# Three heads of the last projection group by twelve GpSimd transfers, dealt over the 16 DMA engines

## The chip, the cores and the metric

One core of one Trainium2 chip. The metric is the device time of one execution in microseconds, the median over runs. Each run also lists the span of that execution, from its first to its last recorded instruction.

## The reference, cut to what matters

A decode step for 4 sequences: `xn = layernorm(x)`; a query projection; attention of 32 query heads over the last 1024 positions of an 8-head cache; an output projection `wo` (4096 x 512); beside it a gated MLP; `out = x + s * g`. Nearly everything read is weights and cache, 28.8 MB, each byte once. The part that changes is the end of the `wo` product:

```python
s = o.reshape(B, Sq, Hq * Dh) @ wo     # wo: 4096 x 512; a group of 4 heads is 512 rows
g = silu(mlp(xn)); return x + s * g
```

## The kernel before

The program builds one list of operations for each engine; SyncE (SP) issues nearly all loads, 28 of 33. The rows of `wo` for group 7, the last of eight, are loaded in two ways: heads 0 to 2 (384 rows) in two even transfers that come last of all, head 3 (128 rows) early, in two small transfers that the trace shows on only 5 and 3 of the 16 DMA engines.

```python
    R3 = (7 * 512 + 384) * D
    d_wox = [pg.dma("sp", "wox%d" % p0, lambda e, p0=p0, n=n, b0=b0: e.dma_start(
        wox_sb[p0:p0 + 4 * n, :, :].rearrange("p j o -> p (j o)"),
        bass.AP(A_wo.tensor, R3 + b0 * D, [[4 * D, n], [4 * n * D, 4], [1, 4 * D]])),
        t_q) for p0, n, b0 in ((0, 5, 0), (32, 3, 80))]
    # ... groups 0 to 6 of wo, then:
    w3_r = A_wo[7 * 512:7 * 512 + 384, :].rearrange("(p i) o -> p i o", i=3)
    d_w3 = [(i0, i1, pg.dma("sp", "w3%d" % i0, lambda e, i0=i0, i1=i1: e.dma_start(
        wo_sb[:, 7, i0:i1, :], w3_r[:, i0:i1, :]))) for i0, i1 in ((0, 2), (2, 3))]
```

The rows land scattered over partitions, so small matmuls with 0/1 matrices (`sel3`, `selx`, built by GpSimd) bring the attention output into the same order. GpSimd otherwise builds masks and issues one transfer:

```python
    c_fold = add("gp", lambda e: e.memset(fold[:, :], 0.0))
    for k in range(4):
        c_fold = add("gp", lambda e, k=k: e.affine_select(...), c_fold)
    # ... x16: 12 rows by ACT, 4 rows by GpSimd
```

The softmax here doesn't subtract the row's maximum and nothing guards it: scores larger than these inputs give would overflow.

## Time and profile before

| | before |
|---|---|
| median time | 76.76 us (three runs, 76.57 to 76.77) |
| span in the profile | 75.05 us |
| time minus span | 1.72 us |
| HBM read | 28.85 MB, 384 GB/s over the span |
| GpSimd: instructions on the page / records in the trace | 24 / 39 |

The page counts only the instructions that keep an engine busy; the trace's records include waits, register moves and drains. The prediction shows the lines on which the reading rests. Three things are to be seen: the DMA engines hardly idle until 70 us (8 or 9 tenths busy in every slice from the second to the thirty-seventh, a share of 1.02 at 70.00 to 70.25); seven of the 16 end by 70.2 us and eight at 71.2 or later; the last matmuls wait for the last transfer.

### The profile page before, as it was taken

The numbers are of one execution on the slowest core, as the hardware profiler recorded it, in microseconds if no ns is written. First come the engines' busy times: TensorE is split into PE (matmuls) and PEld (weight loads), VectorE is DVE, ScalarE is ACT, GpSimd is POOL, SyncE is SP. The second block draws the span as 40 slices with busy tenths as digits, with TensorE's granted clock in tenths as the row PEclk, the third lists the DMA queues.
The fourth block names the chain that finished last, engine by engine and source line by source line (L and its number), as shares of the span: only waits on it lengthen the run. The fifth ranks groups of instructions, "written<-read, shape, count | busy, mean of one in ns | idle before, by whom it ended". The sixth has DMA issues, their size and how long they took to land.

```text
span 75.0 us, 2351 instructions
## 1 busy us (share of the span) xinstructions
PE 51.5 (69%) x1045; PEld 41.3 (55%) x1045; DVE 40.6 (54%) x85; ACT 12.5 (17%) x21; POOL 8.5 (11%) x24
## 2 busy tenths in 40 slices
PE   0000650959999999299999969870869976784670
PEld 0000300259899998299999739640359555573640
DVE  0778200036879997099999606999601664610020
ACT  0611000090003303300330326550030000000000
POOL 6999630000000000000000000000000000000000
PEclk9999999999999999999999999855555555555555
DMA  0999999999999989999999999999999999999700
GB/s 20 262 419 422 430 445 402 420 428 437 419 475 391 466 380 415 432 424 428 424 432 432 415 419 473 401 420 422 424 424 419 419 413 426 421 421 417 277 13 2
DMA packets 4281, 28.94 MB, mean 386 GB/s; under 512 B 526, under 2 KB 658, under 8 KB 1715
## 3 DMA queue, kind: packets, MB, share of 16 engines
q1 hardware_dynamic: 4200, 28.84, 92.3%
q8 instruction: 5, 0.08, 0.4%
q10 hardware_dynamic: 42, 0.01, 0.1%
q0 software_dynamic: 32, 0.00, 0.0%
q14 instruction: 2, 0.01, 0.0%
HBM read 28.85 MB, written 0.00 MB: 384 GB/s over the span
## 4 chain that ended last, share of the span: by engine, by line
PE 22%; DMA 22%; SPq 6%; DVE 3%; ACT 2%; issue 1%
DMA wo_sb<-in_A_wo_dram 22%; PE psK L398 10%; SPq L676 6%; PE psS L418 4%; PE psO L437 2%; PE psK L529 1%; PE psS L444 1%; PE psS L414 1%; DVE kt_buf L539 1%; DVE den_sb L454 1%; PE psM L692 1%; ACT P_buf L426 1%; ACT kt_buf L538 1%; PE psS L714 1%; PE psK L533 0%
## 5 line engine op out<-in xcount | busy, mean ns | idle before, releaser
L404 DVE COPY kt_buf<-psK 128x1024 bf16<-128x1024 bf16 x32 | 20.8, 689 | 3.9 <-PE psK L398 3.9
L398 PE MATMUL psK<-ident,kv_buf 128*128 128x128 bf16 x256 | 20.2, 230 | 1.4 <-PEq L101 1.4
L398 PEld LDWEIGHTS psK<-ident,kv_buf 128*128 128x128 bf16 x256 | 16.2, 104 | 1.5 <-issue 1.4
L418 PE MATMUL psS<-qR,kt_buf 128*128 128x16 bf16 x256 | 10.6, 170 | 0.0
L418 PEld LDWEIGHTS psS<-qR,kt_buf 128*128 128x128 bf16 x256 | 9.7, 97 | 1.3 <-issue 0.3
L437 PEld LDWEIGHTS psO<-P_buf,kv_buf 128*128 128x128 bf16 x256 | 7.7, 102 | 3.6 <-issue 1.9
L437 PE MATMUL psO<-P_buf,kv_buf 128*128 128x16 bf16 x256 | 8.0, 173 | 1.6 <-PEq L101 1.3
L426 ACT ACTIVATE P_buf<-psS 128x512 bf16<-128x512 f32 x8 | 4.8, 597 | 21.9 <-PE psS L418 21.9
L454 DVE TENSOR_REDUCE den_sb<-psS 128x16 f32<-128x512 f32 x8 | 5.5, 682 | 1.3 <-PE psS L444 1.2
L692 PE MATMUL psM<-OW,wo_sb 128*128 128x4 bf16 x124 | 4.2, 167 | 2.3 <-DMA wo_sb<-in_A_wo_dram 2.3
L486 PE MATMUL psO<-wq_sb,xT 128*32 128x512 bf16 x32 | 3.8, 627 | 2.9 <-DMA wq_sb<-in_A_wq_dram 2.7
L470 PE MATMUL psS<-ident,xn_bf 4*128 4x4 bf16 x4 | 0.3, 173 | 7.9 <-DVE y_bf L377 7.9
L692 PEld LDWEIGHTS psM<-OW,wo_sb 128*128 128x128 bf16 x124 | 3.8, 105 | 2.8 <-DMA wo_sb<-in_A_wo_dram 2.5
L470 PEld LDWEIGHTS psS<-ident,xn_bf 4*128 4x128 bf16 x4 | 0.2, 114 | 7.9 <-DVE y_bf L377 7.9
L444 PE MATMUL psS<-P_buf,ones_bf 128*128 128x512 bf16 x8 | 4.3, 534 | 0.0
L492 DVE CAST q_sb<-psO 128x512 bf16<-128x512 f32 x1 | 0.7, 691 | 6.5 <-PE psO L486 6.5
L563 PE MATMUL psK<-w_sb,hT 128*4 128x512 bf16 (+1 forms) x14 | 1.9, 623 | 2.6 <-DMA w_sb<-in_B_w_dram 2.6
L486 PEld LDWEIGHTS psO<-wq_sb,xT 128*32 128x32 bf16 x32 | 0.9, 128 | 5.0 <-DMA wq_sb<-in_A_wq_dram 3.6
L414 PE MATMUL psS<-negm,ind 128*128 128x512 bf16 x8 | 3.3, 411 | 0.0
L710 DVE TENSOR_TENSOR sg_sb<-psM,g_sb 128x16 f32<-128x16 f32 x1 | 0.2, 185 | 5.6 <-PE psM L692 5.6
L448 ACT ACTIVATE P_buf<-P_buf 128x512 bf16<-128x512 bf16 x4 | 2.4, 621 | 1.6 <-PE psS L444 1.6
L563 PEld LDWEIGHTS psK<-w_sb,hT 128*4 128x4 bf16 (+1 forms) x14 | 0.6, 107 | 3.4 <-DVE rden L457 3.1
(82 smaller groups left out, 41.9 us busy)
## 6 DMA issues: line engine op xcount, KB each, us to landing
kv_buf<-in_A_k_cache_dram SPq DMA_DIRECT2D x8, 1024.0 KB, 12.4
kv_buf<-in_A_v_cache_dram SPq DMA_DIRECT2D x8, 1024.0 KB, 12.0
wq_sb<-in_A_wq_dram SPq DMA_DIRECT2D x2, 2048.0 KB, 9.6
w_sb<-in_B_w_dram SPq DMA_DIRECT2D x2, 1792.0 KB, 22.1
wo_sb<-in_A_wo_dram SPq DMA_DIRECT2D x3, 1024.0 KB, 16.3
wo_sb<-in_A_wo_dram SPq DMA_DIRECT2D x1, 512.0 KB, 19.0
wo_sb<-in_A_wo_dram SPq DMA_DIRECT2D x1, 256.0 KB, 16.6
wo_sb<-in_A_wo_dram SPq DMA_DIRECT2D x1, 128.0 KB, 14.7
```

Of the source, the lines that this page charges most:

```text
L398: last = pe.transpose(psK[n % NB][:, j * 128:(j + 1) * 128], kv_buf[:, lg, u * UT + j, :], ident[:, :])
L404: cp[r, n] = bank[n % NB] = add("dve", lambda e: e.tensor_copy(kt_buf[:, n % NKT, :], psK[n % NB][:, 0:1024]), t, kt_user[n % NKT], cls="cp")
L414: pe.matmul(psS[lg % 2][:, 0:512], ind[:, :], negm[:, :], start=True, stop=False, skip_group_check=True)
L418: last = pe.matmul(psS[lg % 2][:, c * 16:(c + 1) * 16], kt_buf[:, n % NKT, j * 128:(j + 1) * 128], qR[:, lg * 16:(lg + 1) * 16], start=Fal ...
L426: ex[g] = add("act", lambda e: e.activation(P_buf[:, g, :], psS[lg % 2][:, 0:512], AF.Exp, scale=SCALE), sc[r, n], cls="ex")
L437: last = pe.matmul(pso[:, 0:16], kv_buf[:, NG + lg, c, :], P_buf[:, lg, c * 16:(c + 1) * 16], start=(c == 0), stop=(c == NC - 1))
L444: den[g] = add("pe", lambda pe: pe.matmul(psS[g % 2][:, 0:512], ones_bf[:, :], P_buf[:, lg, :], start=True, stop=True))
L454: v = add("dve", lambda e: e.tensor_reduce(den_sb[:, cs], bass.AP(psS[g % 2], 0, [[512, 128], [1, 16], [16, NC]]), AX.X, ALU.add), den[g])
L486: last = pe.matmul(psO[m // 4][32 * s:32 * s + 32, 0:512], xT[:, c, :], wq_sb[:, c, m * 512:(m + 1) * 512], start=(c == 0), stop=(c == 3), ...
L563: last = pe.matmul(psK[1][32 * i:32 * i + m, 0:1024].bitcast(F32), hT[:, k, 0:m], w2_sb[:, k, :], start=(k < 4), stop=(k >= FC - 4), tile_ ...
L676: d_wo.append((g0, g1, i0, i1, pg.dma("sp", "wo%d" % n, lambda e: e.dma_start(wo_sb[:, g0:g1, i0:i1, :], wo_r[:, g0:g1, i0:i1, :]))))
L692: last = pe.matmul(psM[:, PS_W + c * 4:PS_W + (c + 1) * 4], w[:, c * 128:(c + 1) * 128], o, start=(st and c == 0), stop=sp, skip_group_che ...
```

## The change

The last even transfer shrinks to head 0, and heads 1 to 3 come early in twelve GpSimd transfers whose slowest dimensions (3, 2, 3, 2, 4, 2, twice) add to 32. The intent, as I read it, is that they go round the 16 engines twice. The rows a partition, 5, 3 or 1, then set how much an engine gets, 40, 24 or 8 KB. The engines that an instruction fetch delayed in the kernel before are apparently meant to get little. For room, the ring of transposed K tiles goes from 10 to 8, and the four rows of `x16` that GpSimd loaded go to ACT.

```diff
-    NKT = 10
+    NKT = 8
-        x16[i:n, :], x_r[i:n, :])) for q, i, n in (("act", 0, 12), ("gp", 12, 16))]
+        x16[i:n, :], x_r[i:n, :])) for i, n in ((0, 12), (12, 16))]          # both by ACT
-    d_wox = [... "sp" ... for p0, n, b0 in ((0, 5, 0), (32, 3, 80))]
+    for p0, n, r in ((0, 3, 5), (12, 2, 3), (20, 3, 1), (64, 2, 1), (72, 4, 5), (88, 2, 1)):
+        XS.append((p0, n, r, b0))
+        b0 += 4 * n * r
+    XS = [(p0 + 32 * h, n, r, b + 192 * h) for h in range(2) for p0, n, r, b in XS]
+    d_wox = [pg.dma("gp", "wox%d" % p0, lambda e, ...: e.dma_start(
+        wox_sb[p0:p0 + 4 * n, 0:r, :].rearrange("p j o -> p (j o)"),
+        bass.AP(A_wo.tensor, R1 + b * D, [[r * D, n], [n * r * D, 4], [1, r * D]])), t_q)
+        for p0, n, r, b in XS]
+    c_sx = add("gp", lambda e: e.memset(selx[:, :, :, :], 0.0))
+    # ... and 14 affine_selects on GpSimd that fill selx (sel3 and its select go)
-    d_w3 = [...]                                # 384 rows, two transfers
+    d_w1st = pg.dma("sp", "w1st", lambda e: e.dma_start(
+        wo_sb[:, 7, 0, :], A_wo[7 * 512:7 * 512 + 128, :]))
```

(The row-selecting matmuls and the projection's small matmuls follow the new layout.)

More of the change, by code (lines that the diff above doesn't have):

```diff
@@ L214, in bass_recurrent_scan__sliding_block_cached__mixer_channel_mlp__decode_kernel @@
     w2_sb = sb([128, FC, D], BF16)
-    wox_sb = wq_sb[0:44, 0, 0:4 * D].rearrange("p (j o) -> p j o", j=4)
+    wox_sb = wq_sb[:, 0, 0:5 * D].rearrange("p (j o) -> p j o", j=5)
     kt_buf = sb([128, NKT, UT * 128], BF16)
@@ L255, in bass_recurrent_scan__sliding_block_cached__mixer_channel_mlp__decode_kernel @@
     OW = sb([128, 4, 28], BF16)
-    sel3 = sb([128, 3, 3, 128], BF16)
-    selx = sb([128, 4, 44], BF16)
-    OW3 = sb([128, 12], BF16)
-    OWx = sb([44, 16], BF16)
+    selx = sb([128, 3, 5, 128], BF16)
+    OWx = sb([128, 20], BF16)
     hT = sb([128, FC, 32], BF16)
@@ L343, in bass_recurrent_scan__sliding_block_cached__mixer_channel_mlp__decode_kernel @@
         base=0, channel_multiplier=-1), c_o32)
-    ones_w = bass.AP(ones_bf, 0, [[128, 128], [0, 9], [1, 128]])
-    c_sel3 = add("gp", lambda e: e.affine_select(
-        sel3[:, :, :, :], ones_w, [[-128, 3], [1, 3], [3, 128]], ALU.is_equal, 0.0,
-        base=0, channel_multiplier=-1), c_1)
-    c_sx = add("gp", lambda e: e.memset(selx[:, :, :], 0.0))
-    for p0, n, b0 in ((0, 5, 0), (32, 3, 80)):
-        c_sx = add("gp", lambda e, p0=p0, n=n, b0=b0: e.affine_select(
-            selx[:, :, p0:p0 + 4 * n], ones_bf[:, 0:16 * n], [[1, 4], [4, n], [4 * n, 4]],
-            ALU.is_equal, 0.0, base=b0, channel_multiplier=-1), c_1, c_sx)
     c_fold = add("gp", lambda e: e.memset(fold[:, :], 0.0))
@@ L365, in bass_recurrent_scan__sliding_block_cached__mixer_channel_mlp__decode_kernel @@
     a = add("act", lambda e: e.activation(sq1[:, :], vt1[:, :], AF.Sqrt), v)
-    d_x16 = [pg.dma(q, "x16%d" % i, lambda e, i=i, n=n: e.dma_start(
-        x16[i:n, :], x_r[i:n, :])) for q, i, n in (("act", 0, 12), ("gp", 12, 16))]
+    d_x16 = [pg.dma("act", "x16%d" % i, lambda e, i=i, n=n: e.dma_start(
+        x16[i:n, :], x_r[i:n, :])) for i, n in ((0, 12), (12, 16))]
     v = add("dve", lambda e: e.reciprocal(rstd1[:, :], sq1[:, :]), a)
@@ L610, in bass_recurrent_scan__sliding_block_cached__mixer_channel_mlp__decode_kernel @@
     mlp1()
-    R3 = (7 * 512 + 384) * D
-    d_wox = [pg.dma("sp", "wox%d" % p0, lambda e, p0=p0, n=n, b0=b0: e.dma_start(
-        wox_sb[p0:p0 + 4 * n, :, :].rearrange("p j o -> p (j o)"),
-        bass.AP(A_wo.tensor, R3 + b0 * D, [[4 * D, n], [4 * n * D, 4], [1, 4 * D]])),
-        t_q) for p0, n, b0 in ((0, 5, 0), (32, 3, 80))]
+    R1 = (7 * 512 + 128) * D
+    XS, b0 = [], 0
+    for p0, n, r in ((0, 3, 5), (12, 2, 3), (20, 3, 1), (64, 2, 1), (72, 4, 5), (88, 2, 1)):
+        XS.append((p0, n, r, b0))
+        b0 += 4 * n * r
+    XS = [(p0 + 32 * h, n, r, b + 192 * h) for h in range(2) for p0, n, r, b in XS]
+    d_wox = [pg.dma("gp", "wox%d" % p0, lambda e, p0=p0, n=n, r=r, b=b: e.dma_start(
+        wox_sb[p0:p0 + 4 * n, 0:r, :].rearrange("p j o -> p (j o)"),
+        bass.AP(A_wo.tensor, R1 + b * D, [[r * D, n], [n * r * D, 4], [1, r * D]])), t_q)
+        for p0, n, r, b in XS]
+    c_sx = add("gp", lambda e: e.memset(selx[:, :, :, :], 0.0))
+    for p0, n, r, b in XS:
+        for j in range(3):
+            if b < 128 * j + 128 and b + 4 * n * r > 128 * j:
+                c_sx = add("gp", lambda e, p0=p0, n=n, r=r, b=b, j=j: e.affine_select(
+                    selx[:, j, 0:r, p0:p0 + 4 * n], ones_bf[:, 0:4 * n * r],
+                    [[1, r], [r, n], [n * r, 4]], ALU.is_equal, 0.0,
+                    base=b - 128 * j, channel_multiplier=-1), c_1, c_sx)
     psx = psS[0]
@@ L638, in fn @@
             o = 7 * 16
-            for a in range(4):
-                last = pe.matmul(psx[0:44, 160 + a * 4:164 + a * 4], selx[:, a, :],
-                                 OTb[:, o + 12:o + 16], start=True, stop=True)
-            for i in range(3):
+            for a in range(5):
                 for j in range(3):
-                    last = pe.matmul(psx[:, 128 + i * 4:132 + i * 4], sel3[:, j, i, :],
-                                     OTb[:, o + j * 4:o + j * 4 + 4],
+                    last = pe.matmul(psx[:, 160 + a * 4:164 + a * 4], selx[:, j, a, :],
+                                     OTb[:, o + 4 + 4 * j:o + 8 + 4 * j],
                                      start=(j == 0), stop=(j == 2))
             return last
-        t = add("pe", fn, ep[HKV - 1], c_sel3, c_sx)
-        return [add("dve", lambda e: e.tensor_copy(OWx[:, :], psx[0:44, 160:176]), t),
-                add("dve", lambda e: e.tensor_copy(OW3[:, :], psx[:, 128:140]), t)]
+        t = add("pe", fn, ep[HKV - 1], c_sx)
+        return add("dve", lambda e: e.tensor_copy(OWx[:, :], psx[:, 160:180]), t)
     for g in range(HKV):
@@ L680, in bass_recurrent_scan__sliding_block_cached__mixer_channel_mlp__decode_kernel @@
         load_wo(n, g0, g1, 0, 4)
-    w3_r = A_wo[7 * 512:7 * 512 + 384, :].rearrange("(p i) o -> p i o", i=3)
-    d_w3 = [(i0, i1, pg.dma("sp", "w3%d" % i0, lambda e, i0=i0, i1=i1: e.dma_start(
-        wo_sb[:, 7, i0:i1, :], w3_r[:, i0:i1, :]))) for i0, i1 in ((0, 2), (2, 3))]
+    d_w1st = pg.dma("sp", "w1st", lambda e: e.dma_start(
+        wo_sb[:, 7, 0, :], A_wo[7 * 512:7 * 512 + 128, :]))
     def wo(tiles, *deps):
@@ L701, in bass_recurrent_scan__sliding_block_cached__mixer_channel_mlp__decode_kernel @@
         if g0 == 0:
-            row_x, row_3 = rows_last()
-            wo([(wox_sb[:, a, :], OWx[:, a * 4:(a + 1) * 4], False, False) for a in range(4)],
+            row_x = rows_last()
+            wo([(wox_sb[:, a, :], OWx[:, a * 4:(a + 1) * 4], False, False) for a in range(5)],
                row_x, *d_wox)
-    for i0, i1, d in d_w3:
-        t_w = wo([(wo_sb[:, 7, i, :], OW3[:, i * 4:(i + 1) * 4], False, i == 2)
-                  for i in range(i0, i1)], d, row_3)
+    t_w = wo([(wo_sb[:, 7, 0, :], OTb[:, 7 * 16:7 * 16 + 4], False, True)], d_w1st,
+             ep[HKV - 1])
     v = add("dve", lambda e: e.tensor_tensor(
```

## The prediction

Read beside it: "instruction fetch" is my word for a packet of the queues that the profile labels instruction; *k* is the number of engines that a transfer uses, and the engine numbers are my names, since no record names an engine. For the kernel before, the trace's completions bear the slowest dimension out as the count for SyncE's and ScalarE's transfers (3, 4, 5 and 12 completions for dimensions of 3, 4, 5 and 12, besides one at the issue). GpSimd's one transfer shows 16 completions for four rows, so they don't tell its k; that GpSimd's k follows the slowest dimension too, and that its transfers take the engines one after the other, was an assumption. The forecast's sum: -0.18 + 0.09 = -0.09 us, called -0.1. Rival 1 is that GpSimd's transfers put one partition on an engine, as the one in the trace did. And the "table load" at 41.6 us is an 8 KB packet of the instruction queue: ScalarE's two table loads are at 1.96 and 15.69 us.

> **What bounds the kernel now.** I read the page's slices first, then the queue lines, then the end of the chain that ended last, then the DMA share of the last two microseconds in quarter-microsecond windows.
>
> ```profile
> DVE  0778200036879997099999606999601664610020
> POOL 6999630000000000000000000000000000000000
> PEclk9999999999999999999999999855555555555555
> DMA  0999999999999989999999999999999999999700
> ...
> q1 hardware_dynamic: 4200, 28.84, 92.3%
> q8 instruction: 5, 0.08, 0.4%
> ```
>
> The DMA row is full from the second slice to the thirty-seventh. The 16 DMA engines never starve, so the span is the start, plus the bytes, plus what happens when the bytes run out. The queue lines show who else uses those engines: five instruction fetches of 16 KB. The POOL row shows that GpSimd has nothing to do after 11 us, so work put there later is free unless someone waits for it.
>
> The chain of waits ends in the output projection's weights:
>
> ```profile
> 55.08 16.56 DMA wo_sb<-in_A_wo_dram
> 71.64 0.05 issue
> 71.68 0.61 PE psM L692 x12
> 72.29 0.03 issue
> 72.32 0.20 DVE sg_sb L710
> ```
>
> So the last two transfers decide the end, and only 12 matmuls and a short tail come after. The windows view (columns: window, its length, busy us of PE, PEld, DVE, ACT, POOL, clock, DMA share, GB/s) shows how the transfers end:
>
> ```profile
> 70.00:70.25 0.25, 0.25 (x16) 0.25 (x14) 0.00 (x0) 0.00 (x0) 0.00 (x0) 0.50 1.02 369
> 70.25:70.50 0.25, 0.25 (x16) 0.25 (x13) 0.00 (x0) 0.00 (x0) 0.00 (x0) 0.50 0.56 221
> 70.50:70.75 0.25, 0.25 (x12) 0.22 (x9) 0.00 (x0) 0.00 (x0) 0.00 (x0) 0.50 0.51 197
> 70.75:71.00 0.25, 0.06 (x3) 0.00 (x0) 0.00 (x0) 0.00 (x0) 0.00 (x0) 0.50 0.53 201
> 71.00:71.25 0.25, 0.21 (x7) 0.21 (x8) 0.00 (x0) 0.00 (x0) 0.00 (x0) 0.50 0.47 168
> 71.25:71.50 0.25, 0.25 (x15) 0.25 (x11) 0.00 (x0) 0.00 (x0) 0.00 (x0) 0.50 0.32 111
> 71.50:71.75 0.25, 0.20 (x7) 0.12 (x5) 0.00 (x0) 0.00 (x0) 0.00 (x0) 0.50 0.04 12
> ```
>
> All engines are busy until 70.2, then the share drops to half at once and stays there until 71.5. Half of the engines finish 1.4 us before the others. This raggedness is all that the change can win: the idle engine time in these rows spread over 16 engines.
>
> The trace's packet records allow more. Within an engine a packet starts 4 ns before the one before it ends, so the packets can be strung into 16 sequences, and all 16 fit what the program gives an engine. I call the four kinds by their load and their end of data. (a) Three engines with 8 packets of 4 KB of the extra wo rows end at 71.36, 71.22 and 71.21. (b) Two with 4 such packets end at 70.54 and 71.41. (c) Seven others end at 70.06 to 70.20. (d) Four others end at 71.48, 71.50, 71.59 and 71.63. Each engine of (d) was hit once by an instruction fetch (at 22.9, 29.2, 48.0, 56.7 us; the packet takes 0.88 to 0.95 us and slows its neighbour, so the engine stays some 1.4 us behind to the end). The later one of (b) was hit by a table load at 41.6. The fifth fetch, at 70.07, fell on an engine of (c) that had just finished. The mean end is 70.80, the last 71.63: perfect balance would give 0.83 us, the upper limit of any such change.
>
> [...] The trace agrees for the hardware queue: the extra rows (slowest dimension 5, then 3) show 5 and 3 engine completions. For GpSimd it shows one transfer only, four 256 B rows on four engines, the same four that hold the input row[...]
>
> **The change, part by part.** Bytes stay the same: the last group's 512 rows of 1 KB. Before, 384 rows come in two even transfers (24 KB an engine) and 128 rows go to engines 0 to 4 (32, 32, 32, 16, 16 KB). After, one even transfer of 128 rows (8 KB an engine) comes last, and the twelve GpSimd transfers add, if their k is 3, 2, 3, 2, 4, 2 twice around: 40 KB on engines 0 to 2 and 10 to 13, 24 KB on 3 and 4, 8 KB on 5 to 9, 14 and 15. So engines 10 to 13 carry 24 KB more and the twelve others 8 KB less. Of (d), two engines are among 12 to 15 and two among 4 to 11 (by whether they took part in a transfer of 12 rows); so the seven light engines are surely meant to be those that fetches hit, and I assume they are.
>
> Per packet the sequences step 42 ns (1 KB), 80 (2 KB), 155 (4 KB), 305 (8 KB), so about 5 ns + 37.6 ns per KB; I estimate 117 for 3 KB and 193 for 5 KB. The cost by engine:
> - Removed everywhere: 8 packets of 2 KB, 0.65 us. Removed on (a): 8 of 4 KB, 1.25; on (b): 4, 0.63.
> - Added: 8 packets of 5 KB, 1.54 us; of 3 KB, 0.94; of 1 KB, 0.34.
> - Added everywhere: GpSimd's small packets. The one such transfer of before put 28 packets of 4 B beside its 4 data packets, two for each engine without data, each 6 ns. Twelve transfers: 12 + 10 packets, 0.13 us.
>
> Sums: (d) -0.65 + 0.34 + 0.13 = -0.18, ends at 71.30 to 71.45. (a) 71.36 - 1.25 - 0.65 + 1.54 + 0.13 = 71.13. (b) 71.41 - 0.63 - 0.65 + 0.94 + 0.13 = 71.20. Engines 10 to 13, from 70.20: -0.65 + 1.54 + 0.13, 71.2. The last end moves from 71.63 to 71.45: the slow four still end last, and they lose only 8 KB.
>
> Then the tail. Before, data ending at 71.63 landed at 71.97, and the last 4 matmuls ended at 72.28, 0.31 later. After, the last transfer is 0.345 us behind group 6 (that is what its 8 packets of 1 KB took before), but group 6's 16 matmuls take 0.43 us from first start to last start. So the last 4 no longer wait for their own data: 0.04 + 0.43 + 4 x 0.027 + 0.17 = 0.75 us after group 6 lands, that is 0.40 after the last landing. The tail grows by 0.09. Net: -0.18 + 0.09, some -0.1 us.
>
> Off the path: 13 row-selecting matmuls become 15, the projection's 28 small matmuls 24, one DVE copy goes; these lie near 66 us, with a wait of 1.5 us for weights after them. At the start GpSimd loses the 1.4 us and 2 x 0.45 us selections. Its new work starts when the q matmuls end (15 us): 12 transfers x 0.7 us (the one of before took 0.68), a memset (about 1.9 us by 528 ns for 512 columns) and 15 selections x 0.4 us, done near 32 us and needed at 65. The smaller K ring (8 of 10) does not bind: a slot is reused 8 units on, scores lag 3.
>
> **The rivals.**
> 1. [...]one partition an engine, always from engine 0. Then engines 0 to 7 carry 32 KB, 8 to 11 22 KB, 12 to 15 10 KB. A slow engine among 5 to 7 gets -0.65 + 1.26 + 0.1 = +0.7, the time some 77.5. For it: the one transfer seen fell on the first four engines. Against: rows and destinations are laid out as if k followed the dimension[...].
> 2. The fetches fall on other engines or at other times, since the instruction streams change. One hit on an engine carrying 40 KB ends near 71.2 + 1.4 = 72.6: 77.7. Against: the code up to the last stage hardly changes, so the first four should stay.
> 3. The small packets cost nothing beside big ones and the tail does not grow: -0.31 us, 76.45.
> 4. GpSimd's work slows the K copies. Before, DVE waits 1.4 us at 30 us for a late K transfer, and the V loads are issued at 46 us for engines that reach them near 50; a delay of 2 us is absorbed. Time unchanged.
>
> **Range and chances.** The main line gives 76.76 - 0.1 = 76.66, say 76.65; I give it some 65%, rival 3 15%, rivals 1 and 2 together 15%. The runs of before spread by 0.2. Range 76.3 to 77.1. Faster by 2% needs 1.5 us, more than perfect balance: 0.01. Slower by 2% needs a fetch on a loaded engine and more: 0.03. Within 2%: 0.96.
>
> **What would show it.** Right: the DMA share falls later but more steeply (above 0.8 until 70.8, gone by 71.5), four engines still end last, the last data 0.1 to 0.3 us earlier, the last 20 matmuls one run. Wrong: engines ending in another pattern (rival 1), a fetch followed by an engine that ends after 72 (rival 2), the DMA row showing a gap in the middle (rival 4).

## The result, and the profile after

| | before | after |
|---|---|---|
| median time | 76.77 us (four runs, 76.57 to 76.78) | 77.03 us (four runs, 76.98 to 77.07) |
| span in the profile | 75.05 us | 75.04 us |
| time minus span, that execution | 1.72 | 2.03 |
| GpSimd: page / records | 24 / 39 | 46 / 61 |

The ratio is 1.004, with a 95% interval of 1.0023 to 1.0058. Ratios here are the mean time of one kernel's fast runs over that of the other's fast runs of the same rounds, so not quite the ratio of the medians. The change is 0.26 us slower, little but clear of noise, and the profiled span did not grow at all.

First the inside of the span. The end of the transfers, in the same windows as before (window, length, busy us of PE, PEld, DVE, ACT, POOL, clock, DMA share, GB/s):

```profile
70.00:70.25 0.25, 0.00 (x0) 0.00 (x0) 0.00 (x0) 0.00 (x0) 0.00 (x0) 0.50 0.81 332
70.25:70.50 0.25, 0.16 (x6) 0.16 (x6) 0.00 (x0) 0.00 (x0) 0.00 (x0) 0.50 0.76 311
70.50:70.75 0.25, 0.25 (x15) 0.25 (x13) 0.00 (x0) 0.00 (x0) 0.00 (x0) 0.50 0.78 311
70.75:71.00 0.25, 0.25 (x15) 0.25 (x13) 0.00 (x0) 0.00 (x0) 0.00 (x0) 0.50 0.67 242
71.00:71.25 0.25, 0.25 (x14) 0.25 (x11) 0.00 (x0) 0.00 (x0) 0.00 (x0) 0.50 0.69 221
71.25:71.50 0.25, 0.11 (x5) 0.02 (x1) 0.00 (x0) 0.00 (x0) 0.00 (x0) 0.50 0.12 41
```

Twelve engines, about three quarters, now work until 71, where it was half before; four end near 70. That is the balance that was intended. The end of the chain of waits (start, us, what):

```profile
52.35 19.17 DMA wo_sb<-in_A_wo_dram
71.52 0.05 issue
71.57 0.70 PE psM L689 x20
72.27 0.02 issue
72.30 0.20 DVE sg_sb L706
```

The last matmuls are now one run of 20 behind group 6's landing, and VectorE's product starts at 72.30 where it started at 72.32. The product won 0.02 us, the whole span 0.01. GpSimd's row on the page and its queue:

```profile
POOL 6994000089999872000000000000000000000000
...
q0 software_dynamic: 608, 0.40, 1.7%
q8 instruction: 5, 0.08, 0.4%
q14 instruction: 1, 0.01, 0.0%
```

Its new work (15 to 29 us) is over long before anyone needs it, and the twelve transfers put 0.40 MB on its queue, 384 rows of 1 KB and small packets. Nothing in these views tells why the execution took 0.3 us longer: that time lies before the first or behind the last instruction record. All four runs show it, with a time minus span of 1.98 to 2.16.

The packed trace holds one thing more that no view prints: semaphore events, and these go on behind the last instruction record. The semaphores from 7 to 255 are each written once there (247 of the 249 have a record in either kernel's trace), and then nine events on semaphore 2 close the execution. In the kernel before, the last four of these nine come 1.81, 1.84, 1.88 and 1.92 us behind the last record; in the changed kernel 1.81, 2.11, 2.14 and 2.19. So 0.26 of the 0.3 us is one late step in that closing exchange, at the very end and not at the start.

### The profile page after: what moved, and what is told of

Read it like the earlier page. It is cut to its first block, busy times and chain, and to the rows that moved or that the text cites. A ratio compares the mean times of both kernels' runs of the same rounds, so it can differ in the third digit from the quotient of the medians.

```text
span 75.0 us, 2371 instructions
## 1 busy us (share of the span) xinstructions
PE 50.3 (67%) x1043; PEld 40.5 (54%) x1043; DVE 40.6 (54%) x84; ACT 12.5 (17%) x21; POOL 17.8 (24%) x46
## 4 chain that ended last, share of the span: by engine, by line
DMA 26%; PE 19%; DVE 3%; SPq 2%; ACT 2%; issue 1%
DMA wo_sb<-in_A_wo_dram 26%; PE psK L383 8%; PE psS L403 4%; PE psO L422 3%; SPq L674 2%; PE psK L514 1%; PE psM L689 1%; PE psS L399 1%; DVE kt_buf L524 1%; DVE den_sb L439 1%; ACT P_buf L411 1%; ACT kt_buf L523 1%; PE psS L429 1%; PE psS L710 1%; PE psK L518 0%
## 5 line engine op out<-in xcount | busy, mean ns | idle before, releaser
L607 POOL DMA_DIRECT2D wq_sb<-in_A_wo_dram x12 | 6.7, 604 | 8.5 <-PE psO L471 8.5
L689 PE MATMUL psM<-OW,wo_sb 128*128 128x4 bf16 x112 | 3.6, 167 | 2.3 <-DMA wo_sb<-in_A_wo_dram 2.3
L689 PEld LDWEIGHTS psM<-OW,wo_sb 128*128 128x128 bf16 x112 | 3.3, 104 | 2.6 <-DMA wo_sb<-in_A_wo_dram 2.5
L615 POOL TENSOR_SCALAR_AFFINE_SELECT selx<-ones_bf 128x8 bf16<-128x8 bf16 (+4 forms) x14 | 4.0, 282 | 1.0
```

The source lines that it names most:

```text
L607: d_wox = [pg.dma("gp", "wox%d" % p0, lambda e, p0=p0, n=n, r=r, b=b: e.dma_start(wox_sb[p0:p0 + 4 * n, 0:r, :].rearrange("p j o -> p (j o)"),
L615: c_sx = add("gp", lambda e, p0=p0, n=n, r=r, b=b, j=j: e.affine_select(selx[:, j, 0:r, p0:p0 + 4 * n], ones_bf[:, 0:4 * n * r], [[1, r], ...
L689: last = pe.matmul(psM[:, PS_W + c * 4:PS_W + (c + 1) * 4], w[:, c * 128:(c + 1) * 128], o, start=(st and c == 0), stop=sp, skip_group_che ...
```

## The experiments

Each job ran the kernel before on the same chip. Over its 42 fast executions in four jobs the mean time minus span was 1.74 to 1.77. The runs list spans to 0.1 us, so means of the difference are good to a few hundredths. The last column is what the theories are about; rows are in the order of the runs.

| kernel | GpSimd records | mean time | mean span | time minus span |
|---|---|---|---|---|
| before (9 runs, first job) | 39 | 76.66 | 74.90 | 1.76 |
| after (4) | 61 | 77.03 | 74.97 | 2.05 |
| one semaphore (5) | 61 | 76.98 | 74.88 | 2.10 |
| spare semaphores (5) | 39 | 76.68 | 74.92 | 1.76 |
| tiny GpSimd transfers (5) | 51 | 76.84 | 75.04 | 1.80 |
| before (11, second job) | 39 | 76.77 | 75.03 | 1.74 |
| 20 memsets first (4) | 59 | 77.03 | 75.00 | 2.03 |
| 2 memsets last (6) | 41 | 76.73 | 75.00 | 1.72 |
| selections first (6) | 61 | 77.01 | 74.97 | 2.04 |
| no GpSimd transfer (4) | 49 | 82.01 | 80.27 | 1.73 |
| before (11, third job) | 39 | 76.78 | 75.05 | 1.74 |
| after, shortened (5) | 47 | 77.36 | 75.60 | 1.76 |
| before, shortened (6) | 26 | 76.76 | 75.02 | 1.74 |
| 16 memsets (2) | 55 | 76.78 | 75.05 | 1.73 |
| 60 memsets (2) | 99 | 76.82 | 75.10 | 1.72 |
| before (11, fourth job) | 39 | 76.77 | 75.00 | 1.77 |
| after, 38 memsets (6) | 99 | 77.41 | 75.67 | 1.74 |

The theories at the start: the 0.3 us outside the span goes with the number of semaphores (S), with the number of GpSimd transfers (G), or with the length of GpSimd's instruction stream (I).

**One semaphore for the twelve** (on the changed kernel).

```diff
-        ... [[r * D, n], [n * r * D, 4], [1, r * D]])), t_q)
+        ... [[r * D, n], [n * r * D, 4], [1, r * D]])), t_q, sem=s_wox)   # waited at 16 * 12
```

> The changed kernel with one semaphore for the twelve GpSimd transfers (11 semaphores fewer than changed, 2 fewer than before); transfers, balance and span unchanged. Theory S (the added time lies outside the profiled span and goes with the number of semaphores: 9 more cost 0.28 us, 0.03 each): span 75.0, time minus span back from 2.03 to about 1.7, time near 76.7. Theory G (it goes with the number of GpSimd transfers) or I (with GpSimd's longer instruction stream): time stays at 77.0.

Measured: 76.96 us median, 2.10 outside. Eleven semaphores fewer bring nothing back: S falls.

**Nine spare semaphores** (on the kernel before).

```diff
+        for i in range(9):
+            nc.alloc_semaphore("spare%d" % i)
```

> The kernel before with nine semaphores allocated and never used, so that the last one has the number it has after the change. Theory S in the form that the highest number or the allocated count matters: 76.77 + 0.28 = 77.05, span unchanged at 75.0. Theory S in the form that only semaphores that are used matter, theories G and I: 76.77.

Measured: 76.70, ratio to before 1.0003, 1.76 outside. S falls from the other side too.

**Twelve tiny GpSimd transfers** (on the kernel before).

```diff
+    d_tiny = [pg.dma("gp", "tiny%d" % i, lambda e, i=i: e.dma_start(
+        tiny[4 * i:4 * i + 4, :], x_r[12:16, :]), sem=s_tiny) for i in range(12)]
```

> The kernel before plus twelve GpSimd transfers of 1 KB each on one semaphore, early, needed by nobody until the end. Their small packets put some 12 x 12 ns on each DMA engine: span up by 0.15. Theory G: time minus span up by 0.3 on top, time near 77.2. Theories S and I (one semaphore more; 12 instructions): 76.9 to 76.95.

Measured: 76.81, the span up by 0.14, 1.80 outside. The small packets cost inside the span what the prediction allowed for them (0.13 to 0.15), and the number of transfers costs nothing outside: G falls.

**Twenty memsets, badly placed** (on the kernel before).

> The kernel before plus twenty short memsets on GpSimd, early, on no path: GpSimd has as many instructions as after the change. Theory I: time minus span up by 0.3, time near 77.05, span 75.0. Theories S and G: unchanged, 76.77.

This kernel was refused by the check ahead of the chip: the memsets all wrote the same bytes, which counts as a race. It did not run; the next does the same with a column each.

The second job set I against two rivals: O, that GpSimd must not end on computation behind transfers, and T, that it is these large transfers themselves.

**Twenty memsets ahead of the transfer** (on the kernel before).

```diff
+    for i in range(20):
+        add("gp", lambda e, i=i: e.memset(junk[:, i:i + 1], 0.0))
```

> The kernel before plus twenty short memsets on GpSimd ahead of its one transfer, so that GpSimd's stream is as long as after the change and a transfer stays its last work. Theory I (the longer stream costs 0.3 us outside the span): time minus span 2.05 instead of 1.77, time near 76.95. Theory O (what counts is that GpSimd's last instruction is computation behind transfers): unchanged, 76.7. Span unchanged at 74.9 in both.

Measured: 77.02, 2.03 outside, ratio 1.0034 (1.0008 to 1.006). Twenty idle memsets of 0.73 us in all, 60 us before the end, on nobody's path, give the whole of the change's loss without any of its transfers. T and O are not needed.

**Two memsets behind the transfer** (on the kernel before, the same two lines below `x16`).

> The kernel before plus two short memsets behind GpSimd's one transfer. Theory O: time minus span 2.05, time near 76.95. Theory I (two instructions more): unchanged, 76.7, minus span 1.77.

Measured: 76.73, 1.72 outside: O falls.

**Selections ahead of the transfers** (the changed kernel's `selx` block moved above `d_wox`).

> The changed kernel with its memset and 14 selections put ahead of the twelve transfers; the same instructions in another order, so transfers are GpSimd's last work as before the change. Theory O: time minus span back to 1.77, span 74.95, time near 76.7. Theory I, or a theory that it is the twelve large transfers themselves (T): stays at 2.07, time 77.0.

Measured: 77.02, 2.04 outside: the order does not matter. As the span was not touched, this run also repeats the balance (below).

**No GpSimd transfer** (the changed kernel with `"gp"` replaced by `"sp"` in `d_wox`).

> The changed kernel with the twelve transfers issued by SyncE instead: no GpSimd transfer at all; [...]384 KB on four engines instead of sixteen, so those end some 3 to 4 us late: span near 78.5. Time minus span: theory T, 1.77; theory O (no transfers before the computation) 1.77; theory I 2.0 (GpSimd still has ten instructions more than before).

Measured: 82.00, span 80.3, 1.73 outside. Each transfer shows 2 to 4 completions besides one at its issue, and the DMA share is 0.42 at 72 to 74 us and 0.17 at 74 to 76, so a few engines carry what sixteen shared. The span grew by 5.3 us where 3 to 4 were expected. Outside it is like before. I had expected 2.0 here by theory I, but with 49 records. If I is a step, it lies above 51 (the tiny transfers) and at or below 59.

The third job asked for the form of the step.

**The changed kernel, shortened**: memsets of five tiles go to VectorE, and one VectorE reduction replaces the memset and four selections of `fold`.

```diff
-    c_xT = add("gp", lambda e: e.memset(xT[:, :, :], 0.0))
+    c_xT = add("dve", lambda e: e.memset(xT[:, :, :], 0.0))         # so yT, zero_bf, ones32, selx
-    c_fold = add("gp", ...)                                         # five instructions
+    c_fold = add("dve", lambda e: e.tensor_reduce(
+        fold[:, :], bass.AP(ident32, 0, [[128, 128], [1, 4], [32, 4]]), AX.X, ALU.add), c_id32)
```

> The changed kernel with ten instructions taken off GpSimd: five memsets (the 1920-column one too) go to VectorE, and the five that build the folding matrix become one VectorE reduction; about 51 GpSimd records in the trace instead of 61. Theory I as a step between 51 and 59 records: time minus span 1.76 instead of 2.05, span 74.95, time near 76.7, level with before or 0.05 below. If the cost grew with each instruction: 1.9, time 76.85. If it belongs to the twelve transfers after all: 2.05, 77.0.

Measured: 1.76 outside with 47 records, as the step says. T, which said 2.05, falls for good, since all twelve transfers are there. But the time was 76.70 and 76.72 in two of five fast runs and 77.77 to 77.83 in three, with spans of 74.9 and 75.0 against 76.0 and 76.1; a sixth run, 77.91 with a span of 76.2, counts as slow. The means in the table mix the two levels. I come back to this.

**The kernel before, shortened** in the same way (without `selx`).

> The kernel before with nine GpSimd instructions moved or folded in the same way; about 30 records instead of 39. Theory I as one step above 51: unchanged, 76.7. If there is another step between 30 and 39: time minus span 1.45, time near 76.4.

Measured: 76.73, ratio 0.9997, 1.74 outside. There is no second step between 26 and 39 records.

**Sixteen and sixty memsets** (on the kernel before, as the twenty).

> The kernel before plus 16 memsets ahead of the transfer, 55 GpSimd records. Theory I as a step: time minus span either 1.76 or 2.05, nothing between; it narrows the step to 52 to 55 or 56 to 59.

> The kernel before plus 60 memsets ahead of the transfer, 99 GpSimd records. A single step: time minus span 2.05. A staircase of equal steps: 2.35 or 2.65. Growth by instruction (0.015 us each from the twenty of before): 2.65. The memsets end near 14 us, ahead of nobody.

Measured: 1.73 outside with 55 records, and 1.72 with 99, in two executions each. The second contradicts I in every form that I had written down: 59 and 61 records cost 0.3 us, 99 cost nothing. The trace of the 99 hints at why. GpSimd in order of time (start, us, engine, line, operation, what ended the idle time), the kernel before and then the one with sixty memsets:

```profile
8.20 1.19 POOL L356 TENSOR_SCALAR_AFFINE_SELECT fold<-fold 128x4 f32<-128x4 f32 x4
9.73 0.68 POOL L366 DMA_DIRECT2D x<-in_A_x_dram  x1 [0.33 <-issue]
```

```profile
9.31 2.08 POOL L363 MEMSET junk<- 128x1 bf16 x60
15.39 0.67 POOL L369 DMA_DIRECT2D x<-in_A_x_dram  x1 [4.00 <-issue]
```

GpSimd stood still for 4.0 us behind its 95th record, waiting for nothing that the profile shows, and in that time, at 13.67 us, the packet records have an instruction packet of 8 KB that no shorter version has at that place. All versions have one such packet at 38.5 to 43.3 us, which the prediction took for a table load. But ScalarE's two table loads in the trace of before are at 1.96 and 15.69 us, and in all 14 traces that packet comes between VectorE's 52nd and 53rd record, also where more VectorE instructions (95 records, not 91) bring it forward from 41.6 to 38.5 us, in the shortened kernel before. So it goes with a place in VectorE's instruction stream. I read GpSimd's stop in the same way, as a wait for its own instruction packet; that is not shown.

So theory F: it matters where GpSimd's stream ends against the place of such a packet. In the run of 99 that place is behind record 95. If what runs behind the kernel's last record counts on from there, 59 or 61 records reach it 34 to 36 places behind their last (an estimate, 95 less 61 or 59), and the semaphore events show that the execution goes on for 1.9 us there. With 99 records the packet comes early, at 13.67 us, where GpSimd has 60 us to spare; with 59 or 61, by F, it comes behind the last record and the end of the execution waits; with 55, 40 places short, the part that is timed ends before it. None of this is shown by the trace of the 99 alone, so the next run tests it.

**The changed kernel with 38 memsets more** (as the twenty, ahead of the transfers).

> The changed kernel plus 38 short memsets early on GpSimd: 99 records instead of 61, more work and not less. Theory F (what costs 0.3 us is where GpSimd's stream ends against an 8 KB block of instruction fetch: 59 to 61 records end just past one, 55 do not reach it, 99 reach it early, while GpSimd is idle anyway): time minus span back from 2.05 to 1.75, span 74.95, time near 76.7, and an 8 KB instruction packet inside the run, near 14 us, as in the run of 99 records before. Theory I (more instructions cost more, the 99 of before an exception): time minus span 2.05 or more, time 77.0 or more.

Measured: 1.74 outside instead of 2.05, by adding work. The page's instruction queue has the second packet now:

```profile
q8 instruction: 5, 0.08, 0.4%
q14 instruction: 2, 0.02, 0.1%
```

Where the changed kernel had one packet of 0.01 MB on that queue, this has two of 8 KB; the new one is at 12.3 us, where near 14 was expected. Two of F's predictions came true, and I's (2.05 or more) did not. At 12.3 us GpSimd was at its 69th record and waiting for the matmuls, so the packet came 26 records ahead of the place where the run of sixty memsets stopped. The 34 to 36 places above stay an estimate.

The semaphore events behind the last record bear on F too. All three traces with 61 records have the late step of 0.30 us, where 0.04 is usual, at the same one of the nine closing events. The eight traces with 26 to 55 records and the two with 99 do not have it. The one with 59 does not have it either, though its execution took 0.26 us longer, so there the delay lies behind the last event. That fits F: with two records fewer in the kernel, the place would come two later behind it. What stays argued and not shown is the fetch itself at the end: the packet records stop with the output transfer (at 74.30 us of 75.05 in the kernel before), ahead of the last instruction record, and the events do not name the engine that was late. That 55 and 99 are free and 59 and 61 are not, in 19 fast executions of four kernels on the dear side, is shown.

The time, though, was 76.64 and 76.83 in two runs and 77.69 to 77.76 in four, again with spans of 74.9 and 75.1 against 76.0.

**What stays open.** Both versions that keep the changed layout and lose the 0.3 us have two levels of span, 1.1 us apart. The granted clock does not separate them: 0.81 to 0.84 on the low level, 0.81 to 0.83 on the high one; in the shortened kernel the high level has the lower clocks, in the other mostly the higher ones. The high level is 1.4% above the low one, just inside the bound of 1.5% from which a run counts as slow, so that these are slow executions of another kind is not excluded. The fifteen executions of the changed layout with its 61 records were all at 74.8 to 75.1, and the kernel before has single executions at 75.4 and 75.7 among 42. The profile fell on the low level both times, so no trace shows the high one. The size fits one thing: a 16 KB instruction fetch in the kernel before put an engine back by 0.88 to 0.95 us for the packet and 0.47 to 0.55 us for its neighbour, 1.4 in all. On an engine with 40 KB, which ends at 71.1, that would make 72.5 instead of 71.4, 1.1 us later. So it may be that where GpSimd's stream ends also moves the 16 KB fetches to other DMA engines, from one execution to the next, away from those that the layout keeps light. That is an estimate, not shown.

No version beat both kernels: the two repaired ones reach 76.64 to 76.83 on their low level, level with before, and lose on the other.

## Why the prediction was right or wrong

The range, 76.3 to 77.1, held 77.03, and "within 2%" was right. The direction was wrong: -0.1 was forecast, +0.26 measured. Neither the main line nor a rival gives 77.03; that the range held it is owed to its width, which is luck.

- **What bounds the kernel, right.** The DMA row is full until 69 us in the traces of both kernels. One reading was loose: the share of one half lasts until 71.25 us in the lines shown, not 71.5.
- **Who gets what, right; rival 1 fell.** In the changed kernel's packet records seven sequences carry the packets of 5 KB and two those of 3 KB rows, as the prediction assumed from the slowest dimensions (3 + 4 for the first, 2 for the second). The sizes show it without any stringing: the 1 KB rows came in 14 packets of 4 KB and the 3 KB rows in 8 of 6 KB, so an engine took rows of several partitions, and rival 1's one partition an engine did not occur. Which engine came first is not recorded; the ends below fit the order that was assumed.
- **The sums by engine, right but for one.** Forecast and measured end of data: the engines hit by a fetch 71.30 to 71.45, and 71.22, 71.25, 71.30, 71.42; the seven with 40 KB 71.1 to 71.2, and 70.97 to 71.24; the mean 70.93, and 70.89. The engine hit by what was called the table load was put at 71.20 and ended at 71.55, last of all. In the run with the selections first, with the same transfers, it ended at 71.37 and the hit ones at 71.21 to 71.36. So the last end moved by 0.08 instead of 0.18 us. One count was off as well: 22 small packets an engine were foreseen, and the trace has 530 in all, 33 an engine. The ends are certain; which end belongs to which kind of engine rests on the stringing into sequences, which the records do not name.
- **The tail, right.** It was to grow from 0.31 to 0.40 us behind the last landing; it took 0.40 (71.86 to 72.26), in one run of 20 matmuls as foretold.
- **GpSimd beside the K copies, right.** They took 690 ns each, before 689, with GpSimd at work; the selections were done at 29 us instead of 32.
- **The fetches stay where they were, right within the span of the profiled run (rival 2 fell there).** The five 16 KB packets came at 23.4, 30.3, 48.3, 57.3 and 71.1 us, the last on an engine that had just finished.
- **The step that failed: "The main line gives 76.76 - 0.1 = 76.66".** It took the change of the span for the change of the time and held the 1.72 us outside for a constant. The prediction listed GpSimd's new instructions and found them free because nobody waits for them in the trace. They are free in the trace: the span moved by -0.01 in the profiles and by -0.02 and -0.06 in the two jobs that compare the same transfers. They cost 0.29 to 0.34 us behind it, and twenty memsets that do nothing cost the same.

Rival 2 came nearest in name, "the instruction streams change", but looked for the cost on a DMA engine inside the span. It may still be at work in the high level of the two repaired kernels, which is open.

## What to carry to other kernels

Compare the change of the time with the change of the span before explaining anything in the trace: what lies outside the instruction records is on no page. When a change adds instructions to an engine that is idle, its stream's length can be a cost of its own kind, here with a step and not monotone (0.3 us with 59 or 61 GpSimd records, nothing with 55 or 99); a control with as many idle instructions and nothing else of the change separates it in one run. And in this kernel, bound by transfers, an instruction fetch of 16 KB set its DMA engine back by some 1.4 us, and the four engines so hit ended last in the kernel before (71.48 to 71.63), so a layout tuned to that holds only as long as the fetches stay where they are.
